# A fourth slot of tokens by seven block products, and the order of work around the first slot

## Chip, core and metric

The kernel runs on one core of a Trainium2 chip. The metric is the device time of one execution in microseconds (us); the time before is the median of 3 runs, 550.5 us (548.32 to 551.82).

## What is computed

Eight batches of eight heads attend over 32 memory rows; the result is read as 4608 tokens of 512 numbers and goes through a mixture of 8 experts, of which each token takes one.

```python
a = softmax(phi, axis=2)                       # (8, 8, 576, 32)
k_m = einsum('bhsm,bhsd->bhmd', a, k)          # (8, 8, 32, 64)
v_m = einsum('bhsm,bhsd->bhmd', a, v)
attn = softmax(matmul(q, k_m.T) / 8, axis=-1)  # (8, 8, 576, 32)
x = matmul(attn, v_m) as (4608, 512)
e_idx = argmax(x @ w_gate, axis=1)
for e in range(8):                             # w1 (512, 1024), w2 (1024, 512)
    mask = e_idx == e
    h = maximum(x[mask] @ w1[e], 0)
    out[mask] = gate_w[mask] * eom[mask, e] * (h @ w2[e])
```

`gate_w` is the chosen expert's softmax probability, `eom` a sigmoid of `x @ w_output_gate`.

## The kernel before

**Attention** runs over 4 pairs of batches, each in 5 steps. `attention` goes through a written order (`ORDER`) for 20 steps `t`, each kind of work with a lag: `C` scores on PE into PSUM (`bpd`), `S` (`shift`) a 32x32 transpose on DVE into `ea`, its maximum `mx` (L855) and the subtraction on POOL (L857), `X` the exponential on ACT (L861), `D` (`divide`) the sum `sa` on DVE and the product on POOL (L872), `B` a transpose back (`aT`), `V0` and `V1` the product with the values on PE (L890), copied by ACT (`xo`, L892) and stored by SP to the table `xs` in DRAM. `M` steps through the memory side (`kvm`, `kT`, `vT`, `ve_b`) of the next pair. `W`, at step 16, splits the first blocks of w.

**Routing** counts and ranks tokens as pairs end. After the second pair `route_early` fills the first 4 slots of 576 tokens each (index lists `idx_ga`, `idx_oa`) and starts the fetches of w; after the last pair `route_late` fills the other 4 (`idx_gl`, `idx_ol`) and up to 28 rests of 128 tokens, which run only if used (in the profiled execution they were not).

**Slots.** A slot is 576 tokens of one expert. POOL gathers its rows from `xs` in five indirect DMAs into `xg` (L468); there is one `xg` buffer. All matmuls take operands split into a high part (float32r) and a low part, in three passes (hh, lh, hl). In a *plain* slot, `turn_x` turns the tokens by 20 PE transposes (L1108, L1113), ACT writes the high parts `xh` and DVE the low parts `xl`; `plain` then makes 192 product matmuls (L1278), 48 for each of four w1 blocks, and `nine` 112 matmuls with the w2 blocks (L1409). In a slot of *seven*, the product with w1 is made from seven half-size products (P1 to P7, 168 matmuls, L1306): SP relays the gathered rows into `xq` by 16 DMAs, DVE turns them in 32x32 squares and makes differences, POOL and DVE make sums of w blocks (S1 to S4), ACT and DVE split more pieces, and `keep` buffers hold partial sums. Before, slots 0 to 3 (`WHOLE`) are plain and 4 to 7 (`SEVEN`) are of seven. What a slot of seven needs (sums, relays, squares, splits) is issued while the slot ahead of it runs: the relays at its product steps 5 and 8, the rest in `nine`.

**Blocks of w.** `Stream.fetch` has SP load 512 KB blocks into 5 raw buffers (7 after `reopen`), up to `cap` ahead of those set free; `split` has ACT write a block's high half (L564) and hands the low half (L569, DVE, two inputs) to `flush`, which issues it and sets the raw block free. `reopen` ends late routing, closes its memory and opens the pool `st` in which seven's buffers lie.

**Queues.** Each engine runs its instructions in the order in which the program issues them, and SP its DMAs likewise. The code above is generated step by step, so that order is decided by where each generator is stepped: `hook` is called between products and steps attention (`att`), routing (`rou`, `late`), gathers and relays.

Of the kernel before, what the change touches and what calls it, by code (L numbers as in the profile page):

```python
# [12 lines left out]
ALU = mybir.AluOpType  # L13
# [3 lines left out]
P = 128  # L17
B, H, S, D, M = 8, 8, 576, 64, 32
# [12 lines left out]
NPE, NPL, NSS = 4, 4, 28  # L31
# [8 lines left out]
START = 17  # L40
# [3 lines left out]
NRAW, CAP = 5, 3  # L44
# [18 lines left out]
EXTRA7 = (2, 6, 9, 12, 17, 19)  # L63
GATHER = {8: 2, 12: 2, 16: 1}
LAST = 1
OPEN = 3
WHOLE = tuple(range(NPE))
SEVEN = tuple(range(NPE, NPE + NPL))
PROD = ("P1", "P2", "P6", "P5", "P3", "P7", "P4")
SPLITS = {"P1": (0, 2), "P6": (2,), "P5": (0, 2)}  # L70
SUMS = {"P6": "S2", "P5": "S1", "P3": "S4", "P7": "S3"}
# [9 lines left out]
def attention_moe(tc, phiT, kv, qT, wgo, wall, out):  # L81
# [3 lines left out]
    with contextlib.ExitStack() as ctx:  # L85
# [185 lines left out]
        def route_early():  # L271
# [29 lines left out]
            known(*order[0:NPE])  # L301
            yield
            yield from hold(LATE["w"])
            stream.fetch()
            t1, t2 = yield from lookup(nch, exc[:], ie[:])
            while 1 not in ranked:
# [8 lines left out]
            for z in order[0:NPE]:  # L315
                z["listed"] = True
            gathers(0, to=1)
            yield

        def route_late():  # L320
# [89 lines left out]
        env = {}  # L410
# [81 lines left out]
        class Stream:  # L492
# [54 lines left out]
                self.sums.add((i, k))  # L547
                return True

            def split(self, ahead, must=False, wait=False):  # L550

                self.flush()
                self.fetch()
                m = self.parted
                if m == len(self.items) or m >= self.used + ahead:
                    return False
                i, k = self.items[m]
                u = {"P1": 0, "P2": 1, "P6": "S2", "P5": 0, "P3": 1, "P7": 2, "P4": 3}.get(k, k)
                if k in SUMS and (i, SUMS[k]) not in self.sums and not (must and self.prep(i, SUMS[k])):
                    return False  # L560
                if (i, u) not in self.w:
                    return False
                w, hl = self.w[i, u], ring.tile()
                A.copy(hl[:, 0], w[:])  # L564
                self.hl[m] = hl
                self.parted += 1

                def low():
                    V.tensor_tensor(hl[:, 1], w[:], hl[:, 0].bitcast(F32), ALU.subtract)  # L569
                    self.freed += FREED.get(k, 1)  # L570
                    self.fetch()

                self.low.append(low)
                if not wait:
                    self.flush()
                return True
# [258 lines left out]
        def scores(bp, u):  # L835
# [9 lines left out]
                                 q[64 * g:64 * g + 64, i * n:i * n + n], start=True, stop=True)  # L845
            return {"n": 16 if u < 4 else 8, "sc": sc}

        def shift(z):
            n = z["n"]
            z["ea"] = wk.tile([P, 16, M], F32, name="ea", bufs=NEA)  # L850
            eav, sc = z["ea"][:, 0:n], z["sc"]
            V.transpose(eav.rearrange("p (g a) m -> p g (a m)", g=2), sc[:, :, 0:n * M // 2])
            tick()
            mx = sm.tile([P, 16], F32, name="mx")
            V.tensor_reduce(mx[:, 0:n], eav, axis=AX.X, op=ALU.max)  # L855
            tick()
            G.tensor_tensor(eav, eav, mx[:, 0:n].unsqueeze(2).to_broadcast([P, n, M]), ALU.subtract)  # L857

        def expo(z):
            eav = z["ea"][:, 0:z["n"]]  # L860
# [2 lines left out]
        def divide(z):  # L863
            n = z["n"]
# [4 lines left out]
            V.tensor_tensor(sa[:, 0:n], sa[:, 0:n], eps[:, 0:n], ALU.add)  # L869
            tick()  # L870
            V.reciprocal(sa[:, 0:n], sa[:, 0:n])
            G.tensor_tensor(eav, eav, sa[:, 0:n].unsqueeze(2).to_broadcast([P, n, M]), ALU.mult)  # L872

        def back(z):
            n = z["n"]
# [260 lines left out]
        def attention():  # L1136
# [8 lines left out]
            for t in range(NT + LAG["V"]):  # L1145
                for w in ORDER:
# [7 lines left out]
                            rou.step(int(w[1:]) * (2 if len(left) == 2 else 1))  # L1154
                    elif w == "W":

                        while t == START - 1 and stream.split(2):
                            pass
                    elif w == "V0" and 0 <= g < NT:
                        bp, c = g // 5, g % 5  # L1160
# [347 lines left out]
        def run(st):  # L1508
# [6 lines left out]
                gat[:] = lo, hi  # L1515

            def hook(step, new):
                if step < 16 or not drip.gens:
                    gathers(i)
                if i + 1 < hi and order[i + 1]["seven"]:  # L1520
# [4 lines left out]
                (rou if rou.gens else late).step(HOOK[1])  # L1525

            for i in range(lo, hi):
                if i == OPEN:
                    reopen()
                gathers(i, i + 1, 0)  # L1530
                if i == lo:
                    for c in range(4):
                        turn_x(order[i], c)

                def nxt(c):
                    if i + 1 < hi:
# [68 lines left out]
```

## Time and profile before

| | before |
|---|---|
| median of 3 runs | 550.5 us (548.32 to 551.82) |
| profiled execution, its own time | 550.38 us |
| its span | 548.6 us |
| mean granted clock over the span | 0.969 |
| PE busy | 500.8 us (91%) |
| DVE, ACT, POOL busy | 362.8, 273.0, 175.0 us |
| first product matmul of slot 0 | 124.20 us |
| slots 2, 3, 4 begin | 244.28, 297.59, 348.44 us |
| last matmul begins | 539.52 us |

The span runs from the first to the last event of the profiled execution; its own time is 1.8 us longer. A row of the trace names start, duration, engine, line and operation (out<-in); in square brackets stands how long the engine was idle before and which engine, tile and line released it. Granted clock 1.00 is TensorE at 2.4 GHz, 0.50 is 1.2 GHz; between them a stretch has both.

### The profile page before, as it was taken

The page shows a single profiled execution, that of the slowest core. Times are in us where ns is not written, and L with a number is a line of the kernel's source. Part 1 is how long each engine was busy: PE and PEld are TensorE (multiplying, and loading weights), DVE is VectorE, ACT ScalarE, POOL GpSimd, SP SyncE. Part 2 cuts the span into 40 slices and gives each one's busy share as a digit, 9 for nine tenths or more (in the row PEclk, how much of TensorE's full clock was granted, in tenths as well). Part 3 has the DMA queues.
Part 4 walks back from the last instruction along what each step waited for, and adds up shares of the span by engine and source line. Part 5 has one row for each costly group of instructions (what it writes and reads, how often), then busy time and mean ns, then how long its engine had stood idle before and what let it go on. Part 6 is the DMA issues. An engine that isn't in the chain of part 4 may idle for free. (4 is left out here: it accounts for less than half of the span.)

```text
span 548.6 us, 10934 instructions
## 1 busy us (share of the span) xinstructions
PE 500.8 (91%) x4141; PEld 432.0 (79%) x4141; DVE 362.8 (66%) x802; ACT 273.0 (50%) x526; POOL 175.0 (32%) x202
## 2 busy tenths in 40 slices
PE   3688677759999999999999999999999999999993
PEld 2455445539987899889988998998899899889982
DVE  4387799766971678975424459578779867878500
ACT  4467474254643453243324325576485666648320
POOL 2334465554251233214022315512612350220021
PEclk9969998769999999999999999999999999999998
DMA  8999999976543575317332830891485179130011
GB/s 324 419 375 384 413 374 396 321 279 192 202 128 133 159 271 132 112 42 249 84 118 71 299 84 11 275 245 48 149 260 169 39 235 258 46 106 21 1 49 44
DMA packets 44414, 103.11 MB, mean 188 GB/s; under 512 B 9600, under 2 KB 18880, under 8 KB 43968
## 3 DMA queue, kind: packets, MB, share of 16 engines
q1 hardware_dynamic: 38464, 82.26, 45.3%
q0 software_dynamic: 5888, 20.06, 10.5%
q8 instruction: 34, 0.56, 0.4%
q14 instruction: 28, 0.23, 0.1%
HBM read 77.23 MB, written 20.35 MB: 178 GB/s over the span
## 5 line engine op out<-in xcount | busy, mean ns | idle before, releaser
L1409 PE MATMUL bps<-whl,hh 128*128 128x512 f32 x576 | 173.2, 393 | 0.0
L1409 PEld LDWEIGHTS bps<-whl,hh 128*128 128x128 f32 x576 | 107.5, 188 | 22.6
L569 DVE TENSOR_TENSOR whl<-w,whl 128x1024 fp32r<-128x1024 f32 x72 | 88.1, 1232 | 52.5 <-ACT whl L564 51.9
L1278 PE MATMUL bps<-xh,whl 128*128 128x288 f32 x512 | 105.1, 297 | 0.0
L1409 PE MATMUL bps<-whl,hl 128*128 128x512 f32 x224 | 87.3, 390 | 0.0
L1278 PEld LDWEIGHTS bps<-xh,whl 128*128 128x128 f32 x512 | 83.0, 188 | 1.3 <-issue 0.6
L564 ACT CAST whl<-w 128x1024 fp32r<-128x1024 f32 x72 | 74.6, 1049 | 3.2 <-PE bpc L1409 2.0
L1278 PE MATMUL bps<-xl,whl 128*128 128x288 f32 x256 | 75.5, 295 | 0.0
L1237 POOL DMA_INDIRECT out<-y,idx_oa x20 | 27.3, 1365 | 110.4 <-ACT y L1236 86.9
L1246 ACT ACTIVATE hh<-bps 128x288 fp32r<-128x288 f32 x64 | 26.4, 412 | 57.9 <-PE bps L1278 56.7
L1237 POOL DMA_INDIRECT out<-y,idx_ol x20 | 21.8, 1090 | 101.4 <-ACT y L1236 66.7
L1409 PEld LDWEIGHTS bps<-whl,hl 128*128 128x128 f32 x224 | 42.1, 188 | 8.2
L1278 PEld LDWEIGHTS bps<-xl,whl 128*128 128x128 f32 x256 | 48.3, 189 | 0.1
L1251 DVE SCALAR_TENSOR_TENSOR hl<-bps,hh 128x288 fp32r<-128x288 f32 x64 | 26.9, 421 | 31.7 <-ACT hh L1246 31.6
L1236 ACT ACTIVATE y<-bps,gx 128x512 f32<-128x512 f32 x28 | 19.3, 690 | 49.7 <-PE bps L1409 44.7
L1306 PE MATMUL bpc<-th,whl 128*128 128x288 f32 x192 | 39.7, 295 | 0.0
L1306 PE MATMUL bpc<-xh,whl 128*128 128x288 f32 x192 | 39.7, 295 | 0.0
L892 ACT COPY xo<-bpd 128x576 f32<-128x576 f32 x36 | 22.5, 639 | 25.2 <-PE bpd L890 17.6
L857 POOL TENSOR_TENSOR ea<-ea,mx 128x512 f32<-128x512 f32 (+1 forms) x20 | 19.2, 961 | 43.5 <-DVE mx L855 41.7
L1306 PEld LDWEIGHTS bpc<-xh,whl 128*128 128x128 f32 x192 | 31.3, 188 | 0.2
L1306 PEld LDWEIGHTS bpc<-th,whl 128*128 128x128 f32 x192 | 31.3, 188 | 0.0
L1246 ACT ACTIVATE hh<-keep 128x288 fp32r<-128x288 f32 x48 | 21.1, 446 | 18.8 <-DVE keep L1317 18.8
(263 smaller groups left out, 890.8 us busy)
## 6 DMA issues: line engine op xcount, KB each, us to landing
w<-wall SPq DMA_DIRECT2D x64, 512.0 KB, 5.1
kvt<-kv SPq DMA_DIRECT2D x32, 512.0 KB, 8.2
xs<-xo SPq DMA_DIRECT2D x16, 576.0 KB, 7.0
qt<-qT SPq DMA_DIRECT2D x16, 512.0 KB, 9.1
ph<-phiT SPq DMA_DIRECT2D x3, 1152.0 KB, 11.7
xq<-xg SPq DMA_DIRECT2D x32, 80.0 KB, 4.8
kv<-kv SPq DMA_DIRECT2D x4, 512.0 KB, 9.9
xq<-xg SPq DMA_DIRECT2D x32, 64.0 KB, 3.9
```

Source lines behind the costliest of these rows:

```text
L564: A.copy(hl[:, 0], w[:])
L569: V.tensor_tensor(hl[:, 1], w[:], hl[:, 0].bitcast(F32), ALU.subtract)
L857: G.tensor_tensor(eav, eav, mx[:, 0:n].unsqueeze(2).to_broadcast([P, n, M]), ALU.subtract)
L892: A.copy(xo[:, c % 2], px[:, :, 0:2 * XQ])
L1236: A.activation(y[0:n], py[0:n], AF.Copy, scale=z["g"][0:n, k:k + 1])
L1237: G.indirect_dma_start(out=out, out_offset=bass.IndirectOffsetOnAxis(ap=z["idx"][1][0:n, z["q0"] + k:z["q0"] + k + 1], axis=0), in_=y[0:n] ...
L1246: A.activation(h_[:, j, c:e], src, AF.Relu)
L1251: V.scalar_tensor_tensor(lo, src[:, s0 - c:s1 - c], 0.0, h_[:, j, s0:s1].bitcast(F32), ALU.max, ALU.subtract)
L1278: T.matmul(pb, w[:, b, o:o + P], x[a][:, cc, c * SL // 2:(c + 1) * SL // 2], start=(n == 0), stop=(n == 11))
L1306: T.matmul(pb, w[:, b, o:o + P], z[x][a][:, kc], start=(first and n == 0), stop=(n == 5), skip_group_check=not first)
L1409: T.matmul(py, a, w[:, b, DM * f:DM * f + DM], start=(u == 4 and f == 0 and n == 0), stop=(u == 7 and f == 1 and n == len(ps) - 1))
```

## The change

Slot 3 goes from `WHOLE` to `SEVEN`; `reopen` is called at product step 2 of slot 2 and not at the start of slot 3. With the early lists known, `cap` is 1 until step 15, so that one block of w is fetched there and the next two at step 15. After the first gathers are issued, the next two operations that `shift` and `divide` would give to POOL go to DVE (`free`). The two splits of step 16 no longer issue their low halves; the first is issued ahead of `turn_x` of slot 0, the second behind it.

```diff
--- before.py
+++ after.py
@@ -63,9 +63,9 @@
 EXTRA7 = (2, 6, 9, 12, 17, 19)
 GATHER = {8: 2, 12: 2, 16: 1}
 LAST = 1
-OPEN = 3
-WHOLE = tuple(range(NPE))
-SEVEN = tuple(range(NPE, NPE + NPL))
+OPEN = (2, 2)
+WHOLE = tuple(range(NPE - 1))
+SEVEN = tuple(range(NPE - 1, NPE + NPL))
 PROD = ("P1", "P2", "P6", "P5", "P3", "P7", "P4")
 SPLITS = {"P1": (0, 2), "P6": (2,), "P5": (0, 2)}
 SUMS = {"P6": "S2", "P5": "S1", "P3": "S4", "P7": "S3"}
@@ -301,6 +301,7 @@
             known(*order[0:NPE])
             yield
             yield from hold(LATE["w"])
+            env["cap"] = 1
             stream.fetch()
             t1, t2 = yield from lookup(nch, exc[:], ie[:])
             while 1 not in ranked:
@@ -315,6 +316,7 @@
             for z in order[0:NPE]:
                 z["listed"] = True
             gathers(0, to=1)
+            env["queued"] = 2
             yield
 
         def route_late():
@@ -547,9 +549,10 @@
                 self.sums.add((i, k))
                 return True
 
-            def split(self, ahead, must=False, wait=False):
-
-                self.flush()
+            def split(self, ahead, must=False, wait=False, hold=False):
+
+                if not hold:
+                    self.flush()
                 self.fetch()
                 m = self.parted
                 if m == len(self.items) or m >= self.used + ahead:
@@ -845,6 +848,10 @@
                                  q[64 * g:64 * g + 64, i * n:i * n + n], start=True, stop=True)
             return {"n": 16 if u < 4 else 8, "sc": sc}
 
+        def free():
+            env["queued"] = env.get("queued", 0) - 1
+            return G if env["queued"] < 0 else V
+
         def shift(z):
             n = z["n"]
             z["ea"] = wk.tile([P, 16, M], F32, name="ea", bufs=NEA)
@@ -854,7 +861,7 @@
             mx = sm.tile([P, 16], F32, name="mx")
             V.tensor_reduce(mx[:, 0:n], eav, axis=AX.X, op=ALU.max)
             tick()
-            G.tensor_tensor(eav, eav, mx[:, 0:n].unsqueeze(2).to_broadcast([P, n, M]), ALU.subtract)
+            free().tensor_tensor(eav, eav, mx[:, 0:n].unsqueeze(2).to_broadcast([P, n, M]), ALU.subtract)
 
         def expo(z):
             eav = z["ea"][:, 0:z["n"]]
@@ -869,7 +876,7 @@
             V.tensor_tensor(sa[:, 0:n], sa[:, 0:n], eps[:, 0:n], ALU.add)
             tick()
             V.reciprocal(sa[:, 0:n], sa[:, 0:n])
-            G.tensor_tensor(eav, eav, sa[:, 0:n].unsqueeze(2).to_broadcast([P, n, M]), ALU.mult)
+            free().tensor_tensor(eav, eav, sa[:, 0:n].unsqueeze(2).to_broadcast([P, n, M]), ALU.mult)
 
         def back(z):
             n = z["n"]
@@ -1154,7 +1161,10 @@
                             rou.step(int(w[1:]) * (2 if len(left) == 2 else 1))
                     elif w == "W":
 
-                        while t == START - 1 and stream.split(2):
+                        if t == START - 2:
+                            env["cap"] = CAP
+                            stream.fetch()
+                        while t == START - 1 and stream.split(2, wait=True, hold=True):
                             pass
                     elif w == "V0" and 0 <= g < NT:
                         bp, c = g // 5, g % 5
@@ -1515,6 +1525,8 @@
                 gat[:] = lo, hi
 
             def hook(step, new):
+                if (i, step) == OPEN:
+                    reopen()
                 if step < 16 or not drip.gens:
                     gathers(i)
                 if i + 1 < hi and order[i + 1]["seven"]:
@@ -1525,12 +1537,13 @@
                 (rou if rou.gens else late).step(HOOK[1])
 
             for i in range(lo, hi):
-                if i == OPEN:
-                    reopen()
                 gathers(i, i + 1, 0)
                 if i == lo:
                     for c in range(4):
+                        if c == 0 and st.low:
+                            st.low.pop(0)()
                         turn_x(order[i], c)
+                    st.flush()
 
                 def nxt(c):
                     if i + 1 < hi:
```

On POOL, around slot 0's gathers (`xg` from `xs` by `idx_ga`; `ea` a step's scores, `mx` their maxima, `sa` their sums), before:

```order
L468 DMA xg_1721<-xs_60,idx_ga_79 128x576 x4
L468 DMA xg_1721<-xs_60,idx_ga_79 64x576
L857 TENSOR_TENSOR ea_1738<-ea_1738,mx_1740 128x512
L872 TENSOR_TENSOR ea_1607<-ea_1607,sa_1744 128x256
L857 TENSOR_TENSOR ea_1812<-ea_1812,mx_1814 128x512
L772 TENSOR_TENSOR ve_b_1819<-kvm_1818,hmask_73 128x2x128
L872 TENSOR_TENSOR ea_1738<-ea_1738,sa_1823 128x512
L857 TENSOR_TENSOR ea_1888<-ea_1888,mx_1890 128x512
```

and in the changed kernel:

```order
L470 DMA xg_1717<-xs_60,idx_ga_79 128x576 x4
L470 DMA xg_1717<-xs_60,idx_ga_79 64x576
L864 TENSOR_TENSOR ea_1812<-ea_1812,mx_1814 128x512
L775 TENSOR_TENSOR ve_b_1819<-kvm_1818,hmask_73 128x2x128
L879 TENSOR_TENSOR ea_1734<-ea_1734,sa_1823 128x512
L864 TENSOR_TENSOR ea_1882<-ea_1882,mx_1884 128x512
```

The first subtraction and the first product behind the gathers are gone from POOL; what stands next is the subtraction of the step after (`ea_1812`).

On DVE, from the first low half (`whl` from `w`) to the low parts of slot 0's tokens (`xl`), before:

```order
L569 TENSOR_TENSOR whl_1851<-w_1584,whl_1851 128x1024
L569 TENSOR_TENSOR whl_1856<-w_1586,whl_1856 128x1024
L798 COPY ve_b_1819<-bpa_1861 128x2x16
L852 STREAM_TRANSPOSE ea_1888<-bpd_1871 128x512
L855 TENSOR_REDUCE mx_1890<-ea_1888 128x16
L1014 TENSOR_REDUCE lg_1466<-xo_1837 128x32
L1071 TENSOR_TENSOR xl_1903<-bps_1907,xh_1902 128x512
L1071 TENSOR_TENSOR xl_1903<-bps_1914,xh_1902 128x4x64
```

and in the changed kernel:

```order
L801 COPY ve_b_1819<-bpa_1855 128x2x16
L859 STREAM_TRANSPOSE ea_1882<-bpd_1865 128x512
L862 TENSOR_REDUCE mx_1884<-ea_1882 128x16
L1021 TENSOR_REDUCE lg_1466<-xo_1837 128x32
L572 TENSOR_TENSOR whl_1851<-w_1584,whl_1851 128x1024
L1078 TENSOR_TENSOR xl_1900<-bps_1904,xh_1899 128x512
L1078 TENSOR_TENSOR xl_1900<-bps_1911,xh_1899 128x4x64
L1078 TENSOR_TENSOR xl_1900<-bps_1918,xh_1899 128x512
L1078 TENSOR_TENSOR xl_1900<-bps_1925,xh_1899 128x512
L1078 TENSOR_TENSOR xl_1900<-bps_1932,xh_1899 128x512
L572 TENSOR_TENSOR whl_1853<-w_1796,whl_1853 128x1024
```

The low halves have moved behind the transpose `ea`, its maximum and the sum `lg`, one ahead of the five `xl` and one behind them.

On SP, the first fetches of w, with stores of attention rows (`xs`) and loads of q (`qt`) between them, before:

```order
L522 DMA w_1584<-wall 128x1024
L522 ISA
L522 DMA w_1586<-wall 128x1024
L522 ISA
L522 DMA w_1588<-wall 128x1024
L1006 DMA xs_60<-xo_1620 128x2x576
L660 DMA qt_1674<-qT 128x1024
L1006 DMA xs_60<-xo_1769 128x2x576
L660 DMA qt_1809<-qT 128x512
```

and in the changed kernel:

```order
L524 DMA w_1584<-wall 128x1024
L1013 DMA xs_60<-xo_1616 128x2x576
L663 DMA qt_1670<-qT 128x1024
L1013 DMA xs_60<-xo_1765 128x2x576
L524 ISA
L524 DMA w_1796<-wall 128x1024
L524 ISA
L524 DMA w_1798<-wall 128x1024
L663 DMA qt_1809<-qT 128x512
```

The second and third fetch stand behind two stores of `xs` and a load of `qt`, and ahead of the next `qt`.

## Rows read from the trace of the kernel before

**Rows 1.** The page, part 1: busy time of PE.
```profile
PE 500.8 (91%) x4141; PEld 432.0 (79%) x4141; DVE 362.8 (66%) x802; ACT 273.0 (50%) x526; POOL 175.0 (32%) x202
```

**Rows 2.** Busy time by stretch (start:end, length, each engine, clock, DMA share, GB/s).
```profile
core 0: us, PE busy (x) PEld busy (x) DVE busy (x) ACT busy (x) POOL busy (x), PEclk, DMA share, GB/s
105.00:124.20 19.20, 12.73 (x156) 9.70 (x152) 12.46 (x25) 9.09 (x19) 10.50 (x11) 0.68 0.79 283
124.20:244.28 120.08, 120.08 (x888) 105.05 (x886) 84.97 (x224) 53.14 (x96) 37.25 (x45) 1.00 0.49 154
244.28:297.59 53.31, 53.31 (x325) 48.37 (x324) 21.37 (x42) 20.88 (x37) 11.17 (x10) 1.00 0.40 126
297.59:348.44 50.85, 50.85 (x306) 46.46 (x304) 31.42 (x52) 21.43 (x38) 21.68 (x14) 1.00 0.48 149
348.44:396.26 47.82, 47.82 (x281) 43.41 (x280) 38.68 (x66) 30.00 (x54) 16.73 (x14) 1.00 0.57 167
```

**Rows 3.** In order of time, PE: start, us, engine, line, operation [idle before <-releaser].
```profile
113.65 0.74 PE L779 MATMUL bpa<-ident,kvm 128*128 128x128 f32 x2 [3.81 <-ACT kvm L770]
...
117.76 1.00 PE L1108 MATMUL bps<-ident,xg 128*128 128x128 f32 x4
...
121.41 0.46 PE L1113 MATMUL bps<-ident,xg 64*128 64x64 f32 x4 [2.65 <-DVE ea L852]
...
124.20 0.59 PE L1278 MATMUL bps<-xh,whl 128*128 128x288 f32 x1
```

**Rows 4.** The same, POOL: two gathers of slot 0 and what follows.
```profile
109.34 1.00 POOL L468 DMA_INDIRECT xg<-xs,idx_ga  x1 [0.30 <-issue]
110.64 0.96 POOL L468 DMA_INDIRECT xg<-xs,idx_ga  x1 [0.31 <-issue]
111.63 1.05 POOL L857 TENSOR_TENSOR ea<-ea,mx 128x512 f32<-128x512 f32 x1
```

**Rows 5.** The same, ACT.
```profile
112.71 0.63 ACT L861 ACTIVATE ea<-ea 128x512 f32<-128x512 f32 x1 [4.25 <-POOL ea L857]
113.25 0.61 ACT L770 ACTIVATE kvm<-pk,rs 128x128 f32<-128x128 f32 x2
...
117.19 1.99 ACT L564 CAST whl<-w 128x1024 fp32r<-128x1024 f32 x2
...
119.79 0.57 ACT L1070 CAST xh<-bps 128x512 fp32r<-128x512 f32 x1
```

**Rows 6.** The same, DVE.
```profile
105.82 0.69 DVE L855 TENSOR_REDUCE mx<-ea 128x16 f32<-128x512 f32 x1
...
118.27 2.36 DVE L569 TENSOR_TENSOR whl<-w,whl 128x1024 fp32r<-128x1024 f32 x2 [2.83 <-ACT whl L564]
...
120.65 0.70 DVE L852 STREAM_TRANSPOSE ea<-bpd 128x512 f32<-128x512 f32 x1
...
123.50 0.69 DVE L1071 TENSOR_TENSOR xl<-bps,xh 128x512 fp32r<-128x512 f32 x1 [0.21 <-ACT xh L1070]
```

**Rows 7.** Landing of the gathers issued at 109.34 and at 110.64, by tile.
```profile
DMA to landing us min/median/max: 6.7/6.7/6.7
...
DMA to landing us min/median/max: 5.7/5.7/5.7
```

**Rows 8.** SP's DMAs; landing of w issued at 100.31, of xs issued at 108.49.
```profile
100.31 1.46 SPq L522 DMA_DIRECT2D w<-wall  x3
...
108.49 0.38 SPq L1006 DMA_DIRECT2D xs<-xo  x1
...
DMA to landing us min/median/max: 4.1/4.1/4.1
...
DMA to landing us min/median/max: 7.9/7.9/7.9
```

**Rows 9.** In order of time, POOL and DVE: a gather beside a low half.
```profile
300.13 1.52 POOL L468 DMA_INDIRECT xg<-xs,idx_gl  x1 [0.30 <-issue]
...
299.50 1.22 DVE L569 TENSOR_TENSOR whl<-w,whl 128x1024 fp32r<-128x1024 f32 x1 [0.54 <-ACT whl L564]
```

## Prediction

> **What bounds the kernel now.** The page comes first: PE is busy for 500.8 of 548.6 us [rows 1]. An average over stages says little, so the table by stage comes next, cut where a slot's first product matmul starts [rows 2]. From 124.20 to 396.26 us PE is busy for the whole of every stretch, at granted clock 1.00 (the upper of its two levels, 2.4 GHz). There only less work on PE brings the end nearer. In the stretch ahead, 105 to 124.2, PE is busy for 12.73 of 19.20 us at granted clock 0.68, so it ran partly at 1.2 GHz and waited for others: there the chain to the first product sets the time.
>
> That chain is read in the time-ordered rows of PE and then of whoever released it. PE has two waits in it [rows 3]: 3.81 us up to 113.65 for `kvm` (ACT), and 2.65 us up to 121.41 for `ea` L852 (DVE).
> - The first: on ACT `kvm` stands behind an exponential that begins at 112.71 after 4.25 us of waiting for POOL's subtraction L857 [rows 5]. That subtraction begins at 111.63, directly behind the last of slot 0's five gathers [rows 4], though the maximum it needs was there at 105.82 + 0.69 = 106.51 [rows 6].
> - The second: L852 begins at 120.65, behind two low halves that hold DVE from 118.27 to 120.63 [rows 6].
>
> The gathers' own data are the third limit: issued at 109.34 and 110.64 [rows 4], the fourth and fifth landed 6.7 and 5.7 us later [rows 7], at 116.04 and 116.34. PE asked for them at 117.76 [rows 3], so now they are hidden with 1.7 us to spare.
>
> **Part 1: slot 3 by seven products.** The three slots in [rows 2] give the price without a model. Slot 2 (plain, hands over to a plain slot) takes 53.31 us, slot 3 (plain, hands over to a slot of seven) 50.85, slot 4 (seven to seven) 47.82. The change makes slot 2 of the second kind and slot 3 of the third; slots 4 to 7 stay as they are. The saving is 53.31 - 47.82 = 5.49 us: 2.46 in slot 2, whose second half no longer carries the 20 PE transposes of slot 3's tokens, and 3.03 in slot 3, which runs 168 products in place of 192.
>
> What comes in for it: 16 relay DMAs on SP, the four-block sums on POOL and DVE, squares and splits on ACT and DVE. All of it was done for slot 4 inside slot 3, where DVE is busy 31.42 and POOL 21.68 of 50.85 us with PE never idle; slot 2 has DVE at 21.37 and POOL at 11.17 of 53.31, so it has that room [rows 2]. I cost it at nothing, with slot 2's PE work as its cover. If that cover failed, PE would wait at slot 3's first product, and the price is what of the 5.49 us it eats (rival B). The pool that holds the new buffers opens two steps into slot 2 and no longer at slot 3; what each buffer waits for is its own memory's last reader, which belongs to the routing that is emitted before slot 2. Its cost is taken as nothing, with the same cover.
>
> **Part 2: two operations on `ea` move to DVE.** The subtraction (128x512) costs DVE about 0.6 us: two operations of 128x1024 with two inputs take 2.36 us [rows 6], a quarter of that is 0.59. The product (128x256) is 0.3. DVE then has the subtraction done at about 106.51 + 0.6 = 107.1. ACT was free for its exponential at 112.71 - 4.25 = 108.46 [rows 5], so the exponential, and `kvm` behind it, can come 4.25 us earlier. PE had ended its own work ahead of that wait at 113.65 - 3.81 = 109.84 [rows 3], so its rows move by 3.81 us, not more: it would be ready for slot 0's tokens at 117.76 - 3.81 = 113.95. Behind the two operations on DVE stand small ones and a transpose into `aT`, all 0.9 us later; what PE wants of them it reads after `kvm`, so after 109.84, and DVE has over 2 us to spare by then.
>
> The price can fall on the gathers. A gather of five took 1.52 us to issue at 300.13 where a low half (two inputs from SBUF) ran on DVE from 299.50 to 300.72 [rows 9], against 0.96 to 1.00 with other neighbours [rows 4]. The two moved operations now run beside slot 0's gathers. Bounds: nothing, or as much as they last, 0.9 us; I take 0.5, near the one row that shows it. The Trainium skill (SBUF — State Buffer, Who interferes with whom) says that a DVE instruction with two SBUF inputs contends with a GpSimd one that reads SBUF, and infers that descriptor generation, which needs the write side, is spared. By that inference the term would be 0 and the sum 0.5 us lower; the 1.52 us row does not agree with it.
>
> **Part 3: reordered first splits.** The first low half now comes after L852 and its followers, the second after the splits of x. L852 then runs as soon as its scores are there, about 114 us, and the wait of 2.65 us is gone. The second low half is wanted only 48 products later, which at 3.03/24 = 0.13 us each (Part 1) is over 6 us: its 1.2 us is covered.
>
> **Part 4: two blocks of w fetched later.** SP issues them behind the store of `xs` that went out at 108.49 and took 0.38 us [rows 8], so from 108.87, 8 us later than before. What is behind them: on ACT the second cast waits for the second block, and behind that cast stand the exponential, `gx` and every split of x. The block's landing has two bounds in [rows 8]: 4.1 us (a block of the same kind at 100.31) and 7.9 us (the store at 108.49, same size class, same moment). I take 6.7, nearer the second since it shares the moment, less something because 1 MB less is ahead of it: 115.6. From the second cast's start to the first split of x is 119.79 - (117.19 + 1.0) = 1.6 us [rows 5], so x's first split begins at 117.2.
>
> **The first product.** Gathers: first transposes at 116.04 and not at 113.95, four take 1.0 us, and from 121.41 to 124.20 the other sixteen took 2.79 us [rows 3]: 116.04 + 1.0 + 2.79 = 119.8. ACT: 117.2 + 0.6 for the split, 0.7 for the low part that frees the bank [rows 6], 1.0 for the last four transposes gives 119.5. The later counts: 119.8, plus 0.5 for stretched gathers, is 120.3, against 124.20: **3.9 us** earlier. Bounds: if the gathers landed before PE is ready, 113.95 + 3.79 = 117.7, a gain of 6.5; with the block at 7.9 us (116.8) and the gathers stretched by 0.9, about 121.5, a gain of 2.7. After the first product PE is full and all else follows it, so the gain reaches the end.
>
> **The sum.** The profiled execution's own time is 550.38 us (span 548.6, 1.8 around it); the median of the runs is 550.5, so no correction between them. 550.4 - 5.5 - 3.9 = 541.0.
>
> **Rivals.**
> - A, the start gives nothing or little: w or the gathers now come too late, since 1 MB more crosses the DMA queues together with the gathers. If the second block lands 9.9 us after issue, at 118.8, the first split of x begins at 120.4 and the first product at about 123: 550.4 - 5.5 - 1.2 = 543.7; with no gain at all 544.9. For it: the DMA share is 0.79 in that stretch [rows 2] and the gathers become the bound. Against: no row there shows a landing beyond 7.9.
> - B, slot 3 isn't fed in time: its sums or relays come late in slot 2 and PE waits before slot 3's first product. Losing half of Part 1 gives 550.4 - 2.7 - 3.9 = 543.8, all of it 546.5. Against: slot 3 did the same for slot 4 without a gap [rows 2].
> - C, slower: the second block of w blocks ACT. Each us that it lands after 116 delays x and so the first product by one. It costs the 3.9 us at a landing near 120 and the other 5.5 at 125.5, 16.6 us after issue, and from there the kernel is slower: at 20 us it would be 550.4 + 3.4 = 553.8. Against: that is twice the longest row of the stretch.
>
> **Numbers.** Forecast (538.4 to 542.2) 0.70; A 0.16; B 0.10; C 0.04. A measurement of this kernel tells about 1% from no change, which is 5.5 us: faster means under 545.0. Of A nearly all is under it, of B about half: faster 0.87, within 1% 0.10, slower 0.03. Forecast and A hold 0.86; the range from 538.0 to 545.0 takes both in.
>
> **What would show it.** Product matmuls of the plain kind 576 and not 768, PE's transposes of tokens 48 and not 64; slot 2 at 50.9 and slot 3 at 47.8 us; the exponential behind the moved subtraction at about 108.5; first transposes at 116 to 117 released by a gather's DMA, not by POOL or DVE; first product at 120.3. The forecast is wrong if PE has a gap at slot 3's start (B), or if ACT waits for a DMA of w at its second cast past 117 (A, C), or if an engine other than PE sets the pace after 120.

## The result and the profile after

The changed kernel takes 544.23 us in the median of 4 runs (542.34 to 544.78), against 551.16 (548.32 to 552.31) for the kernel before: a ratio of 0.9876, 95% interval 0.983 to 0.9922, so 6.9 us faster. The forecast was 541.0 us, with a range from 538 to 545 that takes rival A in; its own bounds were 538.4 to 542.2. The profiled execution of after is the slowest of its four, 544.78 us with a span of 543.1.

| | before | after |
|---|---|---|
| median | 551.16 us | 544.23 us |
| own time, span of the profiled execution | 550.38, 548.6 us | 544.78, 543.1 us |
| index list of slot 0 ready | 104.87 us | 106.73 us |
| gathers 4 and 5 land | 116.04, 116.34 us | 120.58, 121.18 us |
| first product of slot 0 | 124.20 us | 124.38 us |
| slots 2, 3, 4 begin | 244.28, 297.59, 348.44 us | 245.48, 296.33, 344.16 us |
| last matmul ends | 539.91 us | 535.63 us |

The page's row of PE, and the table by stage, cut where slots begin, with the columns of [rows 2]:

```profile
PE 500.6 (92%) x4097; PEld 430.9 (79%) x4097; DVE 383.1 (71%) x832; ACT 282.6 (52%) x543; POOL 179.1 (33%) x202
```
```profile
105.00:124.38 19.38, 13.92 (x203) 10.59 (x203) 14.46 (x30) 9.31 (x19) 9.51 (x9) 0.68 0.93 321
...
245.48:296.33 50.85, 50.85 (x305) 46.47 (x304) 31.84 (x55) 21.43 (x38) 21.22 (x14) 1.00 0.49 148
296.33:344.16 47.83, 47.83 (x282) 43.42 (x280) 38.69 (x66) 30.00 (x54) 16.44 (x14) 1.00 0.56 166
```

Slots 2 and 3 take 50.85 and 47.83 us with PE full. The stretch ahead of the first product is as long as before (19.38 us against 19.20), and its DMA share has risen from 0.79 to 0.93. PE's product and transpose groups, after (times run, then busy us, mean ns, idle before):

```profile
L1288 PE MATMUL bps<-xh,whl 128*128 128x288 f32 x384 | 80.4, 301 | 0.0
...
L1288 PE MATMUL bps<-xl,whl 128*128 128x288 f32 x192 | 57.2, 298 | 0.0
...
L1115 PE MATMUL bps<-ident,xg 128*128 128x128 f32 x48 | 9.1, 321 | 4.9 <-DMA xg<-xs,idx_ga 4.9
```

384 + 192 = 576 plain products are left and 48 transposes of tokens, and these transposes now wait 4.9 us for the gathers' DMA, where [rows 3] had none of that. PE, ACT, DVE and POOL around the first slot, after, in order of time:

```profile
114.72 0.44 PE L1115 MATMUL bps<-ident,xg 128*128 128x128 f32 x2
118.66 0.48 PE L1115 MATMUL bps<-ident,xg 128*128 128x128 f32 x1 [3.51 <-DMA xg<-xs,idx_ga]
120.58 0.48 PE L1115 MATMUL bps<-ident,xg 128*128 128x128 f32 x1 [1.44 <-DMA xg<-xs,idx_ga]
121.33 0.66 PE L1120 MATMUL bps<-ident,xg 64*128 64x64 f32 x4 [0.27 <-DMA xg<-xs,idx_ga]
...
124.38 0.59 PE L1288 MATMUL bps<-xh,whl 128*128 128x288 f32 x1
```
```profile
109.69 0.64 ACT L899 COPY xo<-bpd 128x576 f32<-128x576 f32 x1 [0.32 <-PE bpd L897]
110.22 0.63 ACT L868 ACTIVATE ea<-ea 128x512 f32<-128x512 f32 x1
...
116.42 1.04 ACT L567 CAST whl<-w 128x1024 fp32r<-128x1024 f32 x1 [0.86 <-DMA w<-wall]
...
120.64 0.20 ACT L1060 COPY gx<-xg 128x4 f32<-128x4 f32 x1 [2.64 <-DMA xg<-xs,idx_ga]
...
121.31 1.08 ACT L1077 CAST xh<-bps 128x512 fp32r<-128x512 f32 x2
```
```profile
106.55 0.18 DVE L261 TENSOR_SCALAR idx_ga<-iv 128x20 int32<-128x20 f32 x1
...
108.40 0.69 DVE L864 TENSOR_TENSOR ea<-ea,mx 128x512 f32<-128x512 f32 x1
...
110.17 0.42 DVE L879 TENSOR_TENSOR ea<-ea,sa 128x256 f32<-128x256 f32 x1
...
116.43 0.72 DVE L859 STREAM_TRANSPOSE ea<-bpd 128x512 f32<-128x512 f32 x1
```
```profile
108.59 1.38 POOL L470 DMA_INDIRECT xg<-xs,idx_ga  x1 [0.31 <-issue]
110.27 1.20 POOL L470 DMA_INDIRECT xg<-xs,idx_ga  x1 [0.30 <-issue]
111.78 1.00 POOL L470 DMA_INDIRECT xg<-xs,idx_ga  x1 [0.30 <-issue]
```

PE is ready for tokens at 114.72 and waits 3.51 and 1.44 us for gathers, then, after 0.27 us more for the fifth, makes the rest of its transposes without a gap. ACT's exponential follows directly on its copies at 110.22 (4.25 us of waiting in [rows 5] are gone), its second cast waits 0.86 us for w, and `gx`, the first reader of the gathered rows, 2.64 us for them. Both waits of [rows 3] are gone, and a third has come: the gathers' data. The landing of the fourth and the fifth (6.7 and 5.7 us in [rows 7]), and SP's transfers around them, w now behind a store as [rows 8] let expect:

```profile
DMA to landing us min/median/max: 8.8/8.8/8.8
...
DMA to landing us min/median/max: 8.1/8.1/8.1
```
```profile
110.35 0.36 SPq L1013 DMA_DIRECT2D xs<-xo  x1
110.92 1.53 SPq L524 DMA_DIRECT2D w<-wall  x2
112.55 0.41 SPq L663 DMA_DIRECT2D qt<-qT  x1
```

All executions must be laid side by side with care: the index list is ready between 104.2 and 108.0 us in the 14 profiles, and they differ ahead of any changed instruction (the granted clock of single stretches between 42 and 98 us lies anywhere from 0.67 to 1.00). So the start is measured below from the end of the index list (L261; after: 106.55 + 0.18) to the first product: 19.33 us before, 17.65 after. The forecast's 120.3 stands for 15.43 on this scale.

### The profile page after: what moved, and what is told of

Read it like the earlier page. It is cut to its first block, busy times and chain, and to the rows that moved or that the text cites. A ratio compares the mean times of both kernels' runs of the same rounds, so it can differ in the third digit from the quotient of the medians.

```text
span 543.1 us, 10910 instructions
## 1 busy us (share of the span) xinstructions
PE 500.6 (92%) x4097; PEld 430.9 (79%) x4097; DVE 383.1 (71%) x832; ACT 282.6 (52%) x543; POOL 179.1 (33%) x202
## 5 line engine op out<-in xcount | busy, mean ns | idle before, releaser
L1288 PE MATMUL bps<-xh,whl 128*128 128x288 f32 x384 | 80.4, 301 | 0.0
L1288 PEld LDWEIGHTS bps<-xh,whl 128*128 128x128 f32 x384 | 63.3, 191 | 1.2 <-issue 0.6
L1288 PE MATMUL bps<-xl,whl 128*128 128x288 f32 x192 | 57.2, 298 | 0.0
L1316 PE MATMUL bpc<-th,whl 128*128 128x288 f32 x240 | 49.6, 295 | 0.0
L1316 PE MATMUL bpc<-xh,whl 128*128 128x288 f32 x240 | 49.6, 295 | 0.0
L1316 PEld LDWEIGHTS bpc<-xh,whl 128*128 128x128 f32 x240 | 39.1, 188 | 0.2
L1316 PEld LDWEIGHTS bpc<-th,whl 128*128 128x128 f32 x240 | 39.1, 188 | 0.0
L1288 PEld LDWEIGHTS bps<-xl,whl 128*128 128x128 f32 x192 | 36.7, 191 | 0.1
L1316 PE MATMUL bpc<-xl,whl 128*128 128x288 f32 x120 | 35.4, 295 | 0.0
L1316 PE MATMUL bpc<-tl,whl 128*128 128x288 f32 x120 | 35.4, 295 | 0.0
```

Source lines behind the costliest of these rows:

```text
L1288: T.matmul(pb, w[:, b, o:o + P], x[a][:, cc, c * SL // 2:(c + 1) * SL // 2], start=(n == 0), stop=(n == 11))
L1316: T.matmul(pb, w[:, b, o:o + P], z[x][a][:, kc], start=(first and n == 0), stop=(n == 5), skip_group_check=not first)
```

## The experiments

Each was timed beside the kernel before (medians of before: 551.97 us for e1 to e4, 551.13 for e5 and e9 to e11, 551.52 for e6 to e8 and e12). "Start" is index list to first product in the one profiled execution.

| kernel | median us | lowest to highest | ratio, 95% interval | start us | gathers 4, 5: issue to landing |
|---|---|---|---|---|---|
| after (first comparison) | 544.23 | 542.34 to 544.78 | 0.9876 [0.983, 0.9922] | 17.65 | 8.8, 8.1 |
| e1_seven_only | 545.63 | 542.26 to 546.95 | 0.9866 [0.9834, 0.9897] | 19.63 | 6.5, 5.8 |
| e2_start_only | 547.16 | 546.75 to 549.84 | 0.9919 [0.9892, 0.9946] | 17.21 | 8.4, 7.7 |
| e3_w_early | 541.64 | 540.45 to 544.09 | 0.9823 [0.9795, 0.985] | 15.59 | 6.7, 6.0 |
| e4_w_late | 542.42 | 540.61 to 543.02 | 0.9821 [0.9795, 0.9848] | 16.19 | 7.6, 6.5 |
| e10_after_again | 543.87 | 542.78 to 545.14 | 0.9853 [0.9826, 0.9881] | 18.36 | 9.0, 8.8 |
| e11_w_early_again | 541.54 | 540.27 to 544.90 | 0.9836 [0.9804, 0.9867] | 15.76 | 7.2, 6.2 |
| e9_w_half | 544.22 | 542.19 to 545.58 | 0.9857 [0.983, 0.9883] | 17.28 | 8.4, 7.7 |
| e5_pool_ops | 545.88 | 543.47 to 548.03 | 0.9896 [0.9865, 0.9926] | 18.20 | 8.8, 8.4 |
| e7_early_pool_ops | 544.51 | 542.56 to 545.67 | 0.9870 [0.9844, 0.9896] | 16.59 | not recorded |
| e8_early_old_splits | 545.82 | 540.84 to 547.09 | 0.9883 [0.9848, 0.9919] | 18.29 | not recorded |
| e6_old_splits | 544.26 | 542.37 to 546.67 | 0.9881 [0.9851, 0.9911] | 18.17 | 8.8, not recorded |
| e12_w_between | 541.94 | 540.26 to 545.46 | 0.9825 [0.98, 0.9849] | 16.28 | not recorded |

**e1_seven_only: the first part alone.** The edit is the before kernel with

```diff
-OPEN = 3
-WHOLE = tuple(range(NPE))
+OPEN = (2, 2)
+WHOLE = tuple(range(NPE - 1))
```

and `reopen` moved into `hook`. 

> The kernel before with Part 1 alone (slot 3 by seven products, reopen in slot 2). Theory: it carries 5.5 us, nearly all of the change: about 0.990 of the kernel before; slot 2 lasts 50.85 us, slot 3 47.83, first product as before, some 19.3 us behind the ready index list. Rival (the start parts carry much of the gain and slot 3 part of it is lost): under 4 us.

Slots 2 and 3 of its profile (columns as in the table by stage):

```profile
247.21:298.05 50.84, 50.84 (x305) 46.46 (x304) 31.83 (x55) 21.43 (x38) 21.17 (x14) 1.00 0.49 148
298.05:345.88 47.83, 47.83 (x281) 43.41 (x280) 38.69 (x66) 30.00 (x54) 16.45 (x14) 1.00 0.57 167
```

That is 5.49 us less than 53.31 + 50.85, with PE full in both. The median falls by 6.3 us, the slots account for 5.5. The interval of the ratio stands for 5.7 to 9.2 us, so a rest of at least 0.2 us is not explained; the start is no part of it, since it is 0.3 us longer than before's.

**e2_start_only: all but the first part.** The changed kernel with

```diff
-OPEN = (2, 2)
-WHOLE = tuple(range(NPE - 1))
+OPEN = 3
+WHOLE = tuple(range(NPE))
```

> The kernel before with the two moved operations, the reordered splits and the later w blocks, slots as before. Theory (the moved w blocks slow the gathers, so the start gains little): 0 to 2 us faster, a ratio of 0.996 to 1.0; from the ready index list to the first product 17.6 us against 19.3; gathers 3 to 5 land 8 us or more after issue. Prediction's term: 3.9 us faster, 15.4 us, landings 6 to 7 us.

4.8 us by the medians, with gathers that again land late (8.4 and 7.7 us). With e1's 6.3 this is more than the 6.9 us of both together. The start of its one profile (17.21) is only 0.4 us better than after's. From the index list to the last matmul the profiles do add up, within 1 us: 435.0 us before, 432.8 here, 430.1 in e1, 428.9 in after. What makes the medians' sum larger lies outside that stretch or is scatter, and stays open.

**e3_w_early: the changed kernel without its fourth part.** All three first blocks of w are fetched together, as before:

```diff
-            env["cap"] = 1
             stream.fetch()
...
-                        if t == START - 2:
-                            env["cap"] = CAP
-                            stream.fetch()
```

> The changed kernel with the three first w blocks fetched together again, as in the kernel before. Theory (1 MB of w beside the gathers costs 2 to 3 us): gathers 3 to 5 land 6 to 7 us after issue, first product 15.0 to 15.8 us behind the index list, 1.5 to 2.5 us faster than the changed kernel, so about 8 to 9 us under the kernel before. Rival (the operations that moved to DVE slow the gathers): landings and first product as in the changed kernel, 8 us and 17.6.

Its median is among the lowest here, and repeated in e11 it is again. PE in e3:

```profile
114.79 0.48 PE L1114 MATMUL bps<-ident,xg 128*128 128x128 f32 x1 [1.19 <-DMA xg<-xs,idx_ga]
116.36 0.47 PE L1114 MATMUL bps<-ident,xg 128*128 128x128 f32 x1 [1.10 <-DMA xg<-xs,idx_ga]
117.12 0.66 PE L1119 MATMUL bps<-ident,xg 64*128 64x64 f32 x4 [0.28 <-DMA xg<-xs,idx_ga]
...
120.18 0.59 PE L1284 MATMUL bps<-xh,whl 128*128 128x288 f32 x1
```

PE still meets the gathers one by one, but the last wait ends at 117.12, 12.5 us behind the index list, against 14.6 in after (121.33 - 106.73). From there to the first product it is 3.06 and 3.05 us. So the whole difference in the start, 17.65 - 15.59 = 2.06 us, is the landing.

**e4_w_late: w behind the gathers.** The same two blocks fetched still later, when the gathers are out, with the second block split behind `turn_x`:

```diff
-                        if t == START - 2:
-                            env["cap"] = CAP
-                            stream.fetch()
...
+            if not lo:
+                env["cap"] = CAP
...
+                    while not lo and st.split(2):
+                        pass
```

> The changed kernel with the second and third w block fetched later still, behind the store that follows the gathers, and the second block cast behind slot 0's tokens. Theory: gathers land 4 to 6 us after issue, first product 14 to 15.5 us behind the index list; the second block lands about 6 us after that store and is needed 6.4 us after the first product, so PE may wait up to 2 us there; in sum 1 to 3 us faster than the changed kernel. Rival (w isn't what slows the gathers): landings stay at 8 us, and PE's wait for the second block makes it slower than the changed kernel.

542.42 us, not told from e3. Landings of 7.6 and 6.5 us are above the 4 to 6 expected, and the start of 16.19 is above the 15.5 expected at most. The fourth and fifth gather land 12.6 and 12.8 us behind the index list, against 13.85 and 14.45 in after and 11.7 and 12.3 in e3.

**e10_after_again and e11_w_early_again: the two beside each other.** The changed kernel, and e3's edit, unaltered. 

> The changed kernel once more, beside the next one on the same chip. Theory (the two blocks of w that go out among the gathers' data delay the gathers): from the index list to the first product 17.6 us as before, the fourth and fifth gather land 8 to 9 us after issue, and the time is about 2 us above that of the kernel which fetches w early. Rival (the 2 us are drift of the earlier part of the program, which differs by up to 3 us between profiles): the two kernels agree within 1 us.

 

> The changed kernel with the three first blocks of w fetched together, once more, beside the changed kernel itself. Theory (w delays the gathers): index list to first product 15.6 us, gathers four and five land 6 to 7 us after issue, time about 2 us under the changed kernel. Rival (drift): no difference beyond 1 us, and the index list to first product differs from the first profile of this kernel by as much as from that of the changed one.

543.87 against 541.54 us: 2.3 us, as 544.23 against 541.64 in the first pair, and starts of 18.36 against 15.76. The ranges overlap in both pairs, but the difference comes twice, each time with a start 2.1 to 2.6 us shorter and earlier landings. Drift ahead of the index list can't make that.

**e9_w_half: half the late bytes.** In the changed kernel:

```diff
-            env["cap"] = 1
+            env["cap"] = 2
```

> Changed kernel with the first two blocks of w fetched early and the third alone later: half of the late bytes (0.5 MB in place of 1 MB). Theory (the bytes beside the gathers delay them, in proportion): gathers four and five land about 7.5 us after issue, index list to first product about 16.6 us, time about 1 us under the changed kernel. Rival 1 (what counts is that ACT's second cast waits for its block, not the gathers): the second block is now early, the whole 2 us come back, 15.6 us. Rival 2 (it is not the bytes but the place of the fetch on SP's queue): as the changed kernel, 17.6 us.

544.22 us, landings of 8.4 and 7.7, a start of 17.28: half the bytes cost as much time as all of them, and most of the start (17.65 and 18.36 with 1 MB late, 15.59 and 15.76 with none). A delay in proportion, at 16.6 us, isn't borne out, though single profiles that differ by 0.7 us can't rule it out. Rival 1, at 15.6, falls, since the second block was early here. Rival 2 is the nearest: what counts is where the fetch stands.

What it does there is seen in the DMA queues, in the 2 us that begin 6 us behind the index list. Queue, kind: packets, MB, share of the 16 engines' time; q0 carries POOL's gathers, q1 what SP issues. Before:

```profile
q1 hardware_dynamic: 205, 0.47, 59.2%
q0 software_dynamic: 102, 0.36, 44.2%
```

After, then e9, then e3:

```profile
q1 hardware_dynamic: 201, 0.57, 94.4%
```
```profile
q1 hardware_dynamic: 289, 0.78, 104.2%
q0 software_dynamic: 6, 0.01, 4.8%
```
```profile
q1 hardware_dynamic: 245, 0.55, 69.7%
q0 software_dynamic: 82, 0.28, 34.6%
```

Before and in e3 the two queues share the engines, and the gathers move 0.36 and 0.28 MB in these 2 us. In after and e9 they move nothing or 0.01 MB, though the third was issued from 110.27 to 111.47 and the fourth from 111.78 on: SP's store of `xs` at 110.35, w at 110.92 and `qt` at 112.55 have the engines. In after the gathers' next data comes only from 114.8 on.

Such a stretch is not after's alone; what differs is where it stands. Before, from 107 to 109 us, with gathers issued at 105.16 and 106.73, q1 moves all there is, and the first gathered data comes 4.1 us after the first issue:

```profile
q1 hardware_dynamic: 324, 0.82, 102.8%
```

In after, from 109 to 111 us, SP's queue moves nothing, since the two blocks aren't there yet, and the first data comes 2.0 us after the first issue:

```profile
q0 software_dynamic: 99, 0.38, 77.7%
```

The packets of the other profiles say the same. Where w is fetched ahead of the index list (before, e1, e3, e11, e7, e8, e12), the first data comes 4.1 to 5.0 us after the first issue, and then never stops for over 0.5 us. Where it is fetched among the gathers (after, e10, e9, e2, e6, e5), the first data comes after 2.0 to 2.4 us and then stops for 0.9 to 2.4 us, behind the second gather or, in e5, the third. In e4, with w behind the gathers, it comes after 2.2 us and never stops so long. So the early fetch has the hold-up at the front of the gathers, while PE mostly has other work, and the late one in their midst, while PE waits for them. The Trainium skill (DMA: Bandwidth & Descriptors, Queues, rings and completion order) says that an engine takes turns between its queues packet by packet. The 2 us in which before and e3 share agree with it; the stretches in which the gathers' queue gets nothing, in before as in after and e9, do not. Why the turn fails to come there no run here shows; the records don't tell when a gather's descriptors were ready.

**e12_w_between: w one step sooner on SP.** In the changed kernel

```diff
-                        if t == START - 2:
+                        if t == START - 3:
```

and the two blocks go out behind the first store of `xs` and ahead of `qt`, 2.7 us before the index list is ready.

> Changed kernel with the two later blocks of w fetched one step sooner on SP: behind the first of the two stores of xs and ahead of qt, so about 1.5 us ahead of the index list and not 4 us behind it. Theory (what counts is whether w's bytes cross before the gathers' data or among them): the gathers land 6 to 7 us after issue, index list to first product 15.6 to 16.2 us, to the last matmul about 426 us, time 541.5, about 2 us under the changed kernel. Rival (any fetch later than together with the first block costs): 17.6 us, 428.8 us, 544.

541.94 us, as e3, though its profiled execution is the slowest of its six. The same 2 us of the queues there, and PE's rows:

```profile
q1 hardware_dynamic: 223, 0.51, 64.7%
q0 software_dynamic: 81, 0.28, 39.0%
```
```profile
119.08 0.33 PE L1115 MATMUL bps<-ident,xg 128*128 128x128 f32 x1 [0.79 <-DMA xg<-xs,idx_ga]
119.72 0.43 PE L1120 MATMUL bps<-ident,xg 64*128 64x64 f32 x4 [0.32 <-DMA xg<-xs,idx_ga]
...
123.10 1.11 PE L1115 MATMUL bps<-ident,xg 128*128 128x128 f32 x4 [1.93 <-DVE xl L1078]
```

The gathers move 0.28 MB again, and PE has the fourth and fifth 11.5 and 12.1 us behind the index list (119.08 and 119.72, less 107.59), as in e3. So it is not the later fetch as such that costs but its bytes beside the gathers. The start of 16.28 is then set by DVE's low parts of x, for which PE waits 1.93 us. One number of the theory is missed: to the last matmul it is 428.0 us and not 426, near the rival's 428.8. Of that, 1.5 us are the first 24 products, which took 5.46 us at a lower clock, against 3.93 in e3.

**e5_pool_ops and e7_early_pool_ops: without the second part, w late and w early.** In the changed kernel (e5) and in e3 (e7):

```diff
-            free().tensor_tensor(eav, eav, mx[:, 0:n].unsqueeze(2).to_broadcast([P, n, M]), ALU.subtract)
+            G.tensor_tensor(eav, eav, mx[:, 0:n].unsqueeze(2).to_broadcast([P, n, M]), ALU.subtract)
...
-            free().tensor_tensor(eav, eav, sa[:, 0:n].unsqueeze(2).to_broadcast([P, n, M]), ALU.mult)
+            G.tensor_tensor(eav, eav, sa[:, 0:n].unsqueeze(2).to_broadcast([P, n, M]), ALU.mult)
```

> Changed kernel without its second part: both operations on ea are on GpSimd again, behind slot 0's gathers. Theory (in the changed kernel the landing of the gathers sets the first product, so this part is covered and only stretches the issue of gathers by 0.58 us): PE is ready for tokens 12.9 us behind the index list as in the kernel before, the fifth gather lands 13.9 us behind it, first product at 13.9 + 3.2 = 17.1 us, so 0.5 us sooner than in the changed kernel; time equal within 1 us. Rival (the part carries its 3.8 us): 20 to 21.5 us and about 3 to 4 us slower than the changed kernel.

 

> The three first blocks of w fetched together, reordered splits, slot 3 by seven, but both operations on ea on GpSimd again: the second part alone is missing from the kernel that fetches w early. Theory (without this part PE has slot 0's scores only about 13 us behind the index list, and VectorE's row of L854, a low half and the low parts of x behind them sets the first product, as in the run with w late and this part missing): index list to first product 18.2 us, to the last matmul 429 us, about 2.5 to 3 us slower than with the part. Rival 1 (by the terms of the prediction, PE ready at 12.9 and 3.8 us more): 16.7 us, 1 us slower. Rival 2 (the gathers hide it): 15 to 15.7 us, no slower.

e5, four rows: a gather, a low half and the low parts of x on DVE, PE's last transposes:

```profile
107.72 1.00 POOL L469 DMA_INDIRECT xg<-xs,idx_ga  x1 [0.30 <-issue]
...
120.57 2.08 DVE L571 TENSOR_TENSOR whl<-w,whl 128x1024 fp32r<-128x1024 f32 x1
122.57 2.20 DVE L1073 TENSOR_TENSOR xl<-bps,xh 128x512 fp32r<-128x512 f32 x4
...
123.31 1.11 PE L1110 MATMUL bps<-ident,xg 128*128 128x128 f32 x4 [1.64 <-DVE xl L1073]
```

The second gather is issued in 1.00 us, as those in [rows 4], where after needs 1.38 beside the moved subtraction: the stretch of 0.58 us is the second part's own. But the first product doesn't come sooner, and the start of 18.20 is neither the theory's 17.1 nor the rival's 20: DVE is late with L854 and all behind it, and PE waits 1.64 us for the low parts of x, which I had not reckoned with. The median (545.88) is 2.0 us above e10, with intervals that overlap. With w early the part is worth 2.9 us by the medians (e7 against 541.6) and 1.0 by the starts (16.59 against 15.59): rival 1's number for the start, the theory's for the time. In the profiles e7 is 2.2 us longer than e3 from the index list to the last matmul, of which 1.2 are slower first products (5.16 us for 24, against 3.93).

**e8_early_old_splits and e6_old_splits: without the third part, w early and w late.** In e3 (e8) and in the changed kernel (e6):

```diff
-                        while t == START - 1 and stream.split(2, wait=True, hold=True):
+                        while t == START - 1 and stream.split(2):
...
-                        if c == 0 and st.low:
-                            st.low.pop(0)()
                         turn_x(order[i], c)
-                    st.flush()
```

> The three first blocks of w fetched together, both operations on ea on VectorE, slot 3 by seven, but the first splits in their old order: the third part alone is missing from the kernel that fetches w early. Theory (with the second part everything ahead of L852's transpose is 3.8 us earlier, and the two low halves then lie under the wait for the gathers): index list to first product 15.5 to 16.2 us, to the last matmul about 426 us, time within 1 us of the kernel with the part. Rival (the part carries the wait of 2.65 us that it was to remove): 18.2 us, 428.6 us, 2 to 2.7 us slower.

 

> Changed kernel without its third part: the first splits in their old order, w late. Theory (the gathers, which land 13.5 to 15 us behind the index list beside the late w, set the first product): index list to first product 17.6 to 18.4 us as in the changed kernel, to the last matmul 428.8 us, time within 1 us of it. Rival (L852 now stands behind two low halves, of which the second needs the late block): 20 us or more, 431 us, about 2.5 us slower.

With w late no time is lost that the medians tell (e6, 544.26 against 544.05, the mean of after's two): the gathers hide most of it, and in its profile PE waits 0.84 us for L858 behind them. With w early it is 545.82, 4.2 us above e3 and e11, with one run of six at 540.84. Rows of ACT, DVE and PE in its profile:

```profile
114.34 0.62 ACT L771 ACTIVATE kvm<-pk,rs 128x128 f32<-128x128 f32 x2 [2.85 <-remote]
...
119.65 2.65 DVE L570 TENSOR_TENSOR whl<-w,whl 128x1024 fp32r<-128x1024 f32 x2 [0.51 <-ACT whl L565]
...
123.08 0.69 PE L1118 MATMUL bps<-ident,xg 64*128 64x64 f32 x4 [2.40 <-DVE ea L857]
```

The wait of [rows 3] is back, 2.40 us for L857 behind two low halves. In this execution ACT's `kvm` also stood 2.85 us for something outside the profile's records (PE's last product for it had ended at 112.16). PE stood idle for 2.01 us by it, which makes all of this later but not the gathers; without that the wait would be near 0.4 us (an estimate, 2.40 - 2.01). So the median speaks for the rival, the one profile does not settle it, and how much of the 4.2 us the third part carries stays open.

## Why the prediction was right and where it was wrong

**Part 1, 5.49 us: right.** 50.85 and 47.83 us where 50.85 and 47.82 were forecast, 576 products, 48 transposes, PE full; DVE 31.84 and POOL 21.22 us busy in slot 2. Rival B falls.

**Part 2: right in its own terms.** On the scale of before (after is 1.86 us late at the index list) the exponential came at 110.22 - 1.86 = 108.36, forecast 108.5, and PE was ready for tokens at 112.86, forecast 113.95. The moved operations took 0.69 and 0.42 us (0.59 and 0.3 forecast), and two gathers 0.38 and 0.20 us longer to issue: 0.58 against the 0.5 taken. The Trainium skill's inference (SBUF — State Buffer, Who interferes with whom) that generating descriptors is spared by such DVE operations would have made it 0; e5, where the operations are on POOL and the gathers take 1.00, shows that it isn't.

**Part 3: right, as far as shown.** No wait for L859 is left in after.

**Part 4: w itself was sized well.** 6.7 us were taken for the second block; ACT had it 116.42 - 110.92 = 5.5 us after issue, and rival C, with ACT held by w, falls.

**The step that failed** is the first product's: "first transposes at 116.04 and not at 113.95", plus 0.5. It carried over the landing of the gathers (6.7 and 5.7 us) into a stretch where I had just put 1 MB beside them. It took 8.8 and 8.1, so the last data came 2.2 us later than forecast, and the start is 17.65 and not 15.43 us. What the sum has behind that data held: from the fourth gather's data at 120.58 to the first product are 3.80 us, forecast 1.0 + 2.79. With w early (e3, e11) the start is 15.59 and 15.76 us and the kernel takes 541.6: the forecast was in effect that of a kernel without Part 4. Rival A had the size (543.7 to 544.9) and the cause (1 MB beside the gathers), but reckoned by w's second block at ACT; it was argued down by the longest landing in the rows of before, where a store and a load of q ran beside the last gathers but no w. The measured 544.23 us lies inside the stated range only because that range takes rival A in; it misses the forecast's own 538.4 to 542.2.

**A second term is this execution's, not shown to be the change's.** The first 24 products took 4.97 us (124.38 to 129.35), against 3.94 before (124.20 to 128.14). The granted clock (the column before the last two) in 6 us around them, before, after, e3 and e10:

```profile
124.00:130.00 6.00, 6.00 (x52) 5.64 (x51) 4.19 (x10) 2.37 (x5) 3.79 (x4) 0.89 0.39 104
```
```profile
124.00:130.00 6.00, 6.00 (x45) 5.64 (x43) 4.53 (x9) 1.91 (x4) 3.60 (x4) 0.68 0.39 119
```
```profile
120.00:126.00 6.00, 6.00 (x53) 5.64 (x52) 5.28 (x11) 2.35 (x5) 3.81 (x4) 0.89 0.34 98
```
```profile
125.30:131.30 6.00, 6.00 (x51) 5.64 (x50) 5.32 (x11) 2.37 (x5) 3.79 (x4) 0.87 0.35 105
```

In after the clock fell during PE's first wait for the gathers (up to 118.66) and was at 0.50, the lower level of 1.2 GHz, from 118 to 126 us; in e3 it is back at 1.00 by 122, and its first 24 products took 3.93 us. The prediction priced waits by their length alone. But e10, the same kernel with waits of 3.10 and 2.69 us, made these products in 4.07 us, and over the 14 profiles they took between 3.8 and 5.5. So a wait can cost this, and that the change must pay it isn't shown.

The profiled execution adds up: 541.0 forecast, + 1.86 (index list, not the change), + 2.2 (landing), + 1.0 (clock, this execution), - 1.2 (the end behind the last matmul, 8.69 us before and 7.47 after; it lies between 7.1 and 9.7 in the 14 profiles, so it is not put down to the change) is 544.9, and it took 544.78. By the medians: 551.16 - 5.49 leaves 545.67, so the start brought 1.4 us and not 3.9.

## What to carry to other kernels

When a fetch is moved, price not only when its own bytes land but whose bytes it now runs beside: a landing time read from the trace holds only for the traffic of that moment. If the transfer that it meets is one that the bound engine waits for, move the fetch ahead of it or behind it, never into it: here the medians of e3, e4 and e12 are 1.5 to 2.7 us below the change's. And when two waits are removed, ask which third one lay hidden 2 us beneath them.

## Unexpected of the hardware

- The gathers' queue moved nothing for 2 us while SP's queue had a store, w and `qt` outstanding, with half the bytes of w as with all (0 and 0.01 MB). Before, it moved nothing from 107 to 109 us, while q1 moved 0.82 MB.
- A wait of PE can cost more than its length: in after the first products behind 3.51 and 1.44 us of waiting ran 1.0 us slower, at granted clock 0.68 in place of 0.89. In e10, the same kernel, they ran only 0.1 us slower behind 3.10 and 2.69 us, at 0.87.
- In e8 ACT's `kvm` stood 2.85 us for something that no record names; in after the same instruction waited 0.58 us, in e3 0.25, each time up to the end of PE's product for it.
